# Chunk 3's diagonal sum taken one inner slice sooner, and its masks put ahead of two remainders, in a two-stage kernel (linear attention, then two mixtures of dense layers)

## The chip, the cores and the metric

One core of a Trainium2 chip runs the whole program. The engines named here are TensorE (PE, with its weight loads PEld), VectorE (DVE), ScalarE (ACT), GpSimd (POOL) and SyncE (SP, which here only issues DMAs). The metric is device time in microseconds (us) from the start to the end of one execution; lower is better.

## The reference, cut to what matters

The input is a linear attention with decay over B=2, H=8, S=768, D=48; its output x (1536 tokens by 384) goes through four experts of width 1024, each weighted by a normalised probability, and then through a dense layer of width 2048 with an ELU.

```python
# attention, per head, step t (d, e: 48 by 48 state)
cur   = (u * k[t])[:, None] * v[t][None, :]
y[t]  = r[t] @ (state + cur)
state = w[:, None] * state + k[t][:, None] * v[t][None, :]
# experts
p = probs / probs.sum(-1)
for e in range(4): out += p[:, e] * (relu(x @ w1[e]) @ w2[e])
# last layer
h = out @ w_in;  g = where(h > 0, h, exp(min(h, 0)) - 1);  return g @ w_out
```

## The kernel before

**Chunks of the attention.** The 768 steps of each of the two sequences are cut in 6 chunks of 128, so there are chunks 0 to 11. r and k of a chunk arrive transposed (tile `rkT`) and are scaled on VectorE by powers of w, two instructions for a chunk (`scale`, L231). TensorE then forms the products k·r of the whole chunk (`s2`, L297, 32 small matmuls) in two PSUM banks. What is above the diagonal is kept and put into a table `A` by two masked copies on VectorE (`s2p`, L304, "the masks" below). The diagonal of `A` is another quantity: u·k·r summed over a head. GpSimd multiplies (`s1u`, L248 and L250, tile `uk`), VectorE sums (L256, the "diagonal sum", tile `a0`), and the sums are spread over a diagonal table, one half of the heads by GpSimd (`s1g`, L260) and the other by ScalarE (`s1e`, four instructions, L266). `s1d` is L256 and L260 together. The masks therefore need three things: `s2` of the chunk, L260 and L266.

**Row of a chunk.** `s3(c)` puts together the output of chunk c: r times the carried state (L368), then, as `more` is set, `s2(c+1)`, then the chunk's own contribution to the state (`s3u`, L319, into a `ph` bank), then `A` times v (L380, 16 matmuls, which need the masks of chunk c). VectorE adds the state (`s3s`, L340), ScalarE copies the output to `yT` (L392), and `s3w` (L352, ScalarE) multiplies the new state by the decay of a chunk. After each odd chunk the pair goes out to HBM (`xd`, two DMAs, L397) and comes back in token layout (`xs`, L401), and `s4` splits it in a high and a low part `xh`, `xl` (L542, L543) for the experts. `s2(c+1)` uses the same two PSUM banks as `s2(c)`, so its first two matmuls wait for the two masked copies of chunk c.

**Experts.** Each float matrix product is made of three products of rounded high and low parts. `layers` runs over expert `u`, a block of tokens `t0`, and an inner slice `f` of 128 hidden units (8 slices). For u=0 the first two blocks have 256 tokens. In a slice, `st1` makes 9 matmuls into a `ph` bank (L742), `evac` lets ScalarE take relu (`hh`, L756) and VectorE the remainder (`hl`, L757), and `st2` of the slice two before makes 9 more (L782). At the end of a slice, `work(0.9)` splits one weight slice: ScalarE rounds it (`wh`, L588), VectorE forms the rest (`wl`, L589), and SP is told to load the raw slice that takes the freed buffer. There are three raw buffers and eight weight slices for u=0; two are split before `layers` begins, and one at the end of each inner slice from then on (#2 in slice 0, #3 in slice 1, and so on).

**What sets the order.** The program runs under a manual schedule: every engine takes its instructions in the order in which the code emits them, and so does SP with its DMAs. The attention is woven into the first three token blocks of u=0 by a table, `plan`, with keys (t0 // 256, f, early). An early entry (E) runs between `st1` and `evac`, a late one (L) between `evac` and `st2`:

```python
after = before(u, t0, f)
ph = self.st1(u, t0, n, f)
if after: after(True)                     # E
pend.append((..., *self.evac(u, n, ph)))
if after: after(False)                    # L
if first: self.st2(*first)
if not u or not BA <= f <= BB: self.work(0.9 if not u else 1.2)
```

In the kernel before, slice 1 (entry `y2`, late) holds row 2, the loads of chunk 5, all of chunk 3's diagonal (`diag(3)` is `s1d`, `s1e` and `s3w`), its keys and the scaling of chunk 4, and then split #3. Slice 2 holds, late, `s2(3)` and the masks of chunk 3. Slice 3 holds row 3 (`out(3)`, with `s2(4)` in it), slice 4 chunk 4's diagonal, masks and keys, slice 5 the scaling of chunk 5, slice 6 chunk 5's diagonal and row 4, slice 7 the scaling of chunk 6 and `s4(3)`, whose `xh` and `xl` the next block's first `st1` reads. `s1u(c+1)`, the product that chunk c+1's sum reads, is part of `keys(c)`.

Of the kernel before, what the change touches and what calls it, by code (L numbers as in the profile page):

```python
# [36 lines left out]
BA, BB = 1, 2  # L37
# [487 lines left out]
class Gen:  # L525
# [364 lines left out]
    def layers(self, tb0, before):  # L890


        pend = []
        for u in range(NU):

            m = 0 if u else 2 * tb0
            for t0, n in [(t, tb0) for t in range(0, m, tb0)] + [(t, TB) for t in range(m, N, TB)]:
                for f in range(NF):
                    after = before(u, t0, f)
                    ph = self.st1(u, t0, n, f)  # L900
                    if after:
                        after(True)
                    first = pend.pop(0) if len(pend) >= (2 if u < NE else 3) else None

                    if first and first[3] == NF - 1:
                        self.st2(*first)
                        first = None
                    pend.append((u, t0, n, f, *self.evac(u, n, ph)))
                    if after:
                        after(False)  # L910
                    if first:
                        self.st2(*first)
                    self.run_later()
                    if not u or not BA <= f <= BB:
                        self.work(0.9 if not u else 1.2)
                    if 0 < u < NE and t0 == 0 and f == 2:
                        self.load_pb(u)
        u, t0, n, f, hh, hl = pend[-1]
        for k, i in ((0, 0), (1, 0), (0, 1), (1, 1), (2, 0), (2, 1), (0, 2), (1, 2), (2, 2)):
            self.st2i(*pend[k], i)  # L920
            if k == 2:
                self.evac2i(u, t0, n, i)
# [13 lines left out]
    def fast(self):  # L936
        tc, nc = self.tc, self.nc
        with ExitStack() as ctx:
            self.setup(ctx)
            actx = ExitStack()  # L940
            at = Fast(self, actx)
# [4 lines left out]
            dp = self.probs_in()  # L946
# [76 lines left out]
            def scale(c):  # L1023
                at.s1h(c, 0)
                at.s1h(c, 1)

            def loads(c):
                load(c)
                if c < NCH:
                    at.load_rk(c)  # L1030

            def diag(c):
                at.s1d(c)
                at.s1e(c)
                at.s3w()

            def keys(c):
                at.s1k(c)
                if c + 1 < NCH:
                    at.s1u(c + 1)  # L1040
# [8 lines left out]
            def y2(c):  # L1049
                at.s3(2)  # L1050
                loads(5)
                self.probs_out(lambda: self.pop.tile([P, TB], F32, tag="po0", name="po0"))
                diag(3)
                keys(3)
                scale(4)

# [9 lines left out]
            def rest(c):  # L1066
# [4 lines left out]
            pb = lambda c: self.load_pb(0, *((0, TB), (TB, N))[c])  # L1071
            E, L = True, False
            plan = {
                (0, 0, L): [(lambda c: self.probs2(dp), 0), (k2, 2), (scale, 3)],
                (0, 1, L): [(y2, 2)], (0, 2, L): [(at.s2, 3), (at.s2p, 3)], (0, 3, L): [(out, 3)],
                (0, 4, L): [(diag, 4), (at.s2p, 4), (keys, 4)], (0, 5, E): [(scale, 5)], (0, 5, L): [(pb, 0)],
                (0, 6, E): [(diag, 5)], (0, 6, L): [(out, 4)],
                (0, 7, E): [(scale, 6)], (0, 7, L): [(at.s4, 3), (diag, 6)], (1, 0, L): [(out, 5)],
                (1, 1, E): [(scale, 7)], (1, 1, L): [(diag, 7)], (1, 2, L): [(out, 6)],
                (1, 3, E): [(scale, 8)], (1, 3, L): [(at.s4, 5), (diag, 8)], (1, 4, L): [(out, 7)],  # L1080
# [118 lines left out]
```

## Time and profile before

| | us |
|---|---|
| median of 3 runs | 657.28 (657.26 to 657.31) |
| the profiled execution, its own time | 655.06 |
| its span, first to last instruction | 653.2 |
| TensorE busy | 639.8 (98%) |
| VectorE, ScalarE, GpSimd busy | 327.9, 234.3, 197.6 |
| mean granted TensorE clock | 0.995 of full |

A timeline row gives the start and the duration of an instruction (or of several of one kind, with their count), its engine and line, what it writes and reads, and in brackets the idle time of its engine just before it with what ended that idle time. A window row gives the busy time of each engine in a stretch and the granted clock of TensorE (1.00 is 2.4 GHz, 0.50 is 1.2 GHz). Instructions of one engine overlap by some tens of ns, so that the next one starts a little before the last one's end. Matmul ends are modelled.

### The profile page before, as it was taken

How to read it: one execution, taken by the hardware profiler on the slowest of the kernel's cores; microseconds unless marked ns; L12 is line 12 of the kernel's file. 1: busy time of each engine (PE TensorE's matmuls, PEld its weight loads, DVE VectorE, ACT ScalarE, POOL GpSimd, SP SyncE). 2: the span in 40 equal slices, each digit the busy share in tenths (PEclk: the TensorE clock that was granted, in tenths of full speed). 3: DMA queues.
4: the chain of work that ended last, by engine and by line, in shares of the span. 5: the costliest groups of instructions: out<-in, count | busy, mean ns of one | idle time of the engine just before them, and what ended most of it. 6: DMA issues, size and time to landing. Idle time of an engine off the chain costs nothing.

```text
span 653.2 us, 9220 instructions
## 1 busy us (share of the span) xinstructions
PE 639.8 (98%) x3699; PEld 532.0 (81%) x3701; DVE 327.9 (50%) x452; ACT 234.3 (36%) x438; POOL 197.6 (30%) x169
## 2 busy tenths in 40 slices
PE   8789999999999999999999999999999999999997
PEld 6678988888888888888888888888888888888885
DVE  7856652355454555554545455566676753112122
ACT  7544443233211122211122112123546464544442
POOL 8734541000012130311130314142764434333331
PEclk9989999999999999999999999999999999999999
DMA  8973552433220224322207232208540342001011
GB/s 244 284 223 112 164 153 99 159 98 121 97 96 2 96 82 137 121 98 96 97 2 264 75 121 94 96 25 314 194 146 25 121 145 97 0 1 50 1 49 53
DMA packets 27736, 72.70 MB, mean 111 GB/s; under 512 B 3283, under 2 KB 8453, under 8 KB 27685
## 3 DMA queue, kind: packets, MB, share of 16 engines
q1 hardware_dynamic: 22784, 59.41, 28.3%
q10 hardware_dynamic: 4900, 12.61, 5.0%
q8 instruction: 31, 0.51, 0.3%
q14 instruction: 21, 0.16, 0.1%
HBM read 55.08 MB, written 16.93 MB: 110 GB/s over the span
## 4 chain that ended last, share of the span: by engine, by line
PE 93%; DMA 3%; DVE 1%; ACT 1%; issue 1%; SPq 0%; DVEq 0%; ACTq 0%
PE ph L742 44%; PE po L782 44%; DMA raw<-in_ws_dram 3%; PE pa L297 1%; PE po L927 1%; PE pa L380 1%; PE ph L319 1%; DVE rkT L231 1%; PE pa L368 1%; PE po L380 0%; SPq L551 0%; ACT A L266 0%; DVE A L304 0%; ACT wS L352 0%; ACT wh L588 0%
## 5 line engine op out<-in xcount | busy, mean ns | idle before, releaser
L742 PE MATMUL ph<-xh,wh 128*128 128x512 f32 (+1 forms) x456 | 171.5, 379 | 0.5 <-ACT xh L542 0.3
L742 PE MATMUL ph<-xh,wl 128*128 128x512 f32 (+1 forms) x456 | 170.9, 378 | 0.0
L782 PE MATMUL po<-hh,wh 128*128 128x512 f32 (+1 forms) x447 | 169.7, 380 | 0.0
L782 PE MATMUL po<-hh,wl 128*128 128x512 f32 (+1 forms) x447 | 168.8, 378 | 0.0
L782 PE MATMUL po<-hl,wh 128*128 128x512 f32 (+1 forms) x447 | 168.8, 378 | 0.0
L756 ACT ACTIVATE hh<-ph 128x512 fp32r<-128x512 f32 (+1 forms) x104 | 58.6, 563 | 255.0 <-PE ph L742 254.8
L757 DVE SCALAR_TENSOR_TENSOR hl<-ph,hh 128x512 fp32r<-128x512 f32 (+1 forms) x104 | 67.4, 648 | 161.5 <-ACT hh L756 161.5
L742 PE MATMUL ph<-xl,wh 128*128 128x512 f32 (+1 forms) x456 | 123.1, 378 | 0.0
L742 PEld LDWEIGHTS ph<-xh,wh 128*128 128x128 f32 x456 | 85.7, 188 | 17.1 <-ACT xh L542 1.0
L742 PEld LDWEIGHTS ph<-xh,wl 128*128 128x128 f32 x456 | 85.8, 188 | 15.8
L769 POOL TENSOR_TENSOR hl<-g,hh 128x512 fp32r<-128x512 f32 x48 | 63.0, 1314 | 117.7 <-ACT hh L768 109.5
L782 PEld LDWEIGHTS po<-hh,wh 128*128 128x128 f32 x447 | 84.0, 188 | 17.1 <-issue 1.5
L782 PEld LDWEIGHTS po<-hl,wh 128*128 128x128 f32 x447 | 84.0, 188 | 15.6
L782 PEld LDWEIGHTS po<-hh,wl 128*128 128x128 f32 x447 | 84.0, 188 | 15.6
L742 PEld LDWEIGHTS ph<-xl,wh 128*128 128x128 f32 x456 | 83.4, 188 | 16.2 <-DVE xl L543 0.2
L652 POOL TENSOR_TENSOR nl<-a,wide 128x768 fp32r<-128x768 f32 x16 | 29.8, 1864 | 188.0 <-DVE a L651 147.2
L766 DVE SCALAR_TENSOR_TENSOR g<-m,ph 128x512 f32<-128x512 f32 x48 | 32.9, 686 | 104.5 <-ACT m L764 99.1
L804 POOL TENSOR_TENSOR acc<-acc,t 128x512 f32<-128x512 f32 x27 | 34.2, 1297 | 72.9 <-DVE t L803 72.9
L768 ACT CAST hh<-g 128x512 fp32r<-128x512 f32 x48 | 29.9, 622 | 43.0 <-DVE g L766 43.0
L763 ACT ACTIVATE m<-ph 128x512 f32<-128x512 f32 x48 | 28.7, 598 | 43.4 <-PE ph L742 36.7
L589 DVE TENSOR_TENSOR wl<-raw,wh 128x768 fp32r<-128x768 f32 x32 | 31.0, 981 | 9.1 <-ACT wh L588 8.6
L764 ACT ACTIVATE m<-m 128x512 f32<-128x512 f32 x48 | 30.3, 632 | 1.5
(134 smaller groups left out, 496.0 us busy)
## 6 DMA issues: line engine op xcount, KB each, us to landing
raw<-in_ws_dram SPq DMA_DIRECT2D x32, 384.0 KB, 4.1
wide<-in_ws_dram SPq DMA_DIRECT2D x16, 768.0 KB, 5.1
w<-nh ACTq DMA_DIRECT2D x16, 384.0 KB, 2.4
w<-nl ACTq DMA_DIRECT2D x16, 384.0 KB, 5.6
wh<-w SPq DMA_DIRECT2D x16, 384.0 KB, 6.2
wl<-w SPq DMA_DIRECT2D x16, 384.0 KB, 6.8
rk<-in_rkv_dram SPq DMA_DIRECT2D x12, 384.0 KB, 5.5
rkT<-in_rkT_dram SPq DMA_DIRECT2D x10, 448.0 KB, 5.4
```

The source lines that it names most:

```text
L589: self.weng.tensor_tensor(out=lo, in0=t, in1=hi.bitcast(F32), op=ALU.subtract)
L652: nc.gpsimd.tensor_tensor(out=lo, in0=af, in1=cf, op=ALU.add)
L742: nc.tensor.matmul(ph[:, 0:n], a[:, kk, c0:c0 + P], b[:, kk], start=q == 0, stop=q == 3 * KD - 1)
L756: nc.scalar.activation(hh[:, 0:n], ph[:, 0:n], AF.Relu)
L757: nc.vector.scalar_tensor_tensor(out=hl[:, 0:n], in0=ph[:, 0:n], scalar=0.0, in1=hh[:, 0:n].bitcast(F32), op0=ALU.max, op1=ALU.subtract)
L763: nc.scalar.activation(m, ph, AF.Relu, scale=-1.0)
L764: nc.scalar.activation(m, m, AF.Exp, scale=-1.0)
L766: nc.vector.scalar_tensor_tensor(out=gg, in0=m, scalar=-1.0, in1=ph, op0=ALU.add, op1=ALU.max)
L768: nc.scalar.copy(hh, gg)
L769: nc.gpsimd.tensor_tensor(out=hl, in0=gg, in1=hh.bitcast(F32), op=ALU.subtract)
L782: nc.tensor.matmul(po, a[:, ff, i * P:(i + 1) * P], b[:, 0:n], start=f == 0 and q == 0 and not i * n % TB, stop=f == NF - 1 and q == 2 and ...
L804: nc.gpsimd.tensor_tensor(out=a, in0=a, in1=t[:, 0:n], op=ALU.add)
```

## The change

Nothing is computed differently; the order of emission changes in the first token block.

- Slice 0, late: `s1d(3)` (sum of chunk 3's diagonal, and GpSimd's half of the table) is added behind the scaling of chunk 3. In slice 1 only `s1e(3)` and `s3w` are left of `diag(3)`.
- Slice 1: no split at its end. Every later split is one slice later: #3 at the end of slice 2, #4 of slice 3, up to #7 of slice 6.
- Slice 2: `s2(3)` and chunk 3's masks are early, so the masks stand ahead of the slice's relu remainder and of the rest of split #3.
- Slice 3: `diag(4)` follows row 3 directly, before `st2` and the split.
- Slice 4: chunk 4's masks and keys are early; the scaling of chunk 5 comes late in this slice and no longer early in the next one.
- Slice 5, late: `diag(5)`, which was early in slice 6.

```diff
-                    if not u or not BA <= f <= BB:
+                    if (t0 or f != 1) if not u else not BA <= f <= BB:
                         self.work(0.9 if not u else 1.2)
...
                 self.probs_out(lambda: self.pop.tile([P, TB], F32, tag="po0", name="po0"))
-                diag(3)
+                at.s1e(3)
+                at.s3w()
                 keys(3)
                 scale(4)
...
-                (0, 0, L): [(lambda c: self.probs2(dp), 0), (k2, 2), (scale, 3)],
-                (0, 1, L): [(y2, 2)], (0, 2, L): [(at.s2, 3), (at.s2p, 3)], (0, 3, L): [(out, 3)],
-                (0, 4, L): [(diag, 4), (at.s2p, 4), (keys, 4)], (0, 5, E): [(scale, 5)], (0, 5, L): [(pb, 0)],
-                (0, 6, E): [(diag, 5)], (0, 6, L): [(out, 4)],
+                (0, 0, L): [(lambda c: self.probs2(dp), 0), (k2, 2), (scale, 3), (at.s1d, 3)],
+                (0, 1, L): [(y2, 2)], (0, 2, E): [(at.s2, 3), (at.s2p, 3)], (0, 3, L): [(out, 3), (diag, 4)],
+                (0, 4, E): [(at.s2p, 4), (keys, 4)], (0, 4, L): [(scale, 5)], (0, 5, L): [(diag, 5), (pb, 0)],
+                (0, 6, L): [(out, 4)],
```

## Rows read from the trace of the kernel before

**Rows 1.** The page: busy time of the engines, share of the span, instructions.

```profile
PE 639.8 (98%) x3699; PEld 532.0 (81%) x3701; DVE 327.9 (50%) x452; ACT 234.3 (36%) x438; POOL 197.6 (30%) x169
```

**Rows 2.** Windows: stretch, length, busy PE PEld DVE ACT POOL, PEclk, DMA, GB/s.

```profile
27.99:31.49 3.50, 0.01 (x3) 0.01 (x1) 2.73 (x4) 2.02 (x5) 3.25 (x3) 1.00 0.91 247
31.49:36.18 4.69, 4.51 (x65) 3.76 (x65) 2.07 (x4) 0.37 (x1) 0.00 (x0) 0.64 0.81 268
...
46.01:50.08 4.07, 4.07 (x64) 3.55 (x65) 2.46 (x6) 1.81 (x6) 2.24 (x3) 0.58 0.73 224
...
60.00:120.00 60.00, 59.85 (x669) 51.98 (x668) 28.07 (x50) 23.02 (x65) 21.04 (x19) 1.00 0.47 141
```

**Rows 3.** Timeline of TensorE, first token block.

```profile
20.65 0.67 PE L319 MATMUL po<-v,kp 128*64 128x48 f32 x16
...
22.50 0.29 PE L714 MATMUL po<-ident,pn 128*48 128x128 f32 x1
...
23.96 1.10 PE L297 MATMUL pa<-rkT 48*64 48x128 f32 x32
...
31.49 0.43 PE L297 MATMUL pa<-rkT 48*64 48x128 f32 x2 [3.49 <-DVE A L304]
...
36.18 0.39 PE L782 MATMUL po<-hh,wh 128*128 128x256 f32 x1
...
38.43 0.28 PE L782 MATMUL po<-hh,wh 128*128 128x256 f32 x1
...
46.01 1.98 PE L297 MATMUL pa<-rkT 48*64 48x128 f32 x32 [2.51 <-DVE rkT L231]
...
50.08 0.39 PE L782 MATMUL po<-hh,wh 128*128 128x256 f32 x1
...
54.75 0.62 PE L742 MATMUL ph<-xl,wh 128*128 128x256 f32 x3
```

**Rows 4.** Timeline of VectorE, same stretch.

```profile
22.37 1.50 DVE L231 TENSOR_TENSOR rkT<-rkT,Kd 112x512 f32<-112x512 f32 x1
...
25.25 0.54 DVE L256 TENSOR_REDUCE a<-uk 128x8 f32<-128x384 f32 x1
...
28.76 1.70 DVE L589 TENSOR_TENSOR wl<-raw,wh 128x768 fp32r<-128x768 f32 x1 [0.92 <-ACT wh L588]
30.39 0.41 DVE L757 SCALAR_TENSOR_TENSOR hl<-ph,hh 128x256 fp32r<-128x256 f32 x1
30.72 1.31 DVE L304 COPY_PREDICATED A<-mask,pa 128x512 f32<-128x512 uint8 x2
31.94 0.93 DVE L589 TENSOR_TENSOR wl<-raw,wh 128x768 fp32r<-128x768 f32 x1
```

**Rows 5.** Timeline of ScalarE, same stretch.

```profile
25.82 1.28 ACT L266 ACTIVATE A<-ident,a 128x128 f32<-128x128 f32 x4 [2.65 <-DVE a L256]
27.01 1.00 ACT L352 ACTIVATE wS<-S,T 112x48 f32<-112x48 f32 x4
27.91 0.82 ACT L588 CAST wh<-raw 128x768 fp32r<-128x768 f32 x1
...
36.33 0.37 ACT L392 COPY yT<-po 112x256 f32<-112x256 f32 x1 [0.18 <-PE po L380]
```

**Rows 6.** Timeline of GpSimd, same stretch.

```profile
21.75 1.56 POOL L250 TENSOR_TENSOR uk<-uk,rk 128x384 f32<-128x384 f32 x1
```

**Rows 7.** Timeline of SP's DMA issues.

```profile
36.73 0.83 SPq L397 DMA_DIRECT2D xd<-yT  x2
41.62 0.39 SPq L401 DMA_DIRECT2D xs<-xd  x1
```

**Rows 8.** DMA issues of the span: KB each, median us to landing.

```profile
raw<-in_ws_dram SPq DMA_DIRECT2D x32, 384.0 KB, 4.1
...
pb<-pd SPq DMA_DIRECT2D x1, 512.0 KB, 8.9
```

**Rows 9.** Waits of SP, 0 to 110 us: total, times, longest.

```profile
SPq L551 <- PE po L368: 11.0, 2, 10.0
```

## The prediction

> **What bounds the kernel now.** I read the page first: TensorE is busy 639.8 us of a span of 653.2 (98%) while VectorE, ScalarE and GpSimd are at 50%, 36% and 30% [rows 1]. So at most some 13 us are to be had, and the windows say where. From 60 us on TensorE is full (59.85 of 60.00) at a granted clock of 1.00 [rows 2]; what is lost lies before that, in the first token block, the block that the diff rearranges. The TensorE timeline shows two standstills there: 3.49 us until 31.49, released by VectorE's masks, and 2.51 us until 46.01, released by VectorE's scaling [rows 3]. Each is followed by a stretch at a lowered clock: 0.64 on average from 31.49 to 36.18, 0.58 from 46.01 to 50.08 [rows 2], a mix of the levels 1.2 and 2.4 GHz. The third view is the timelines of the other engines: which instruction stood in front of the masks. Since everything behind 60 us is full, I carry a time won at the end of block one to the end of the kernel one to one.
>
> What a lowered clock costs: products of a chunk (32 matmuls) take 1.10 us [rows 3], of which 1.04 up to the next start; state share plus A times v take 22.50 - 20.65 = 1.85 [rows 3]. That is 2.9 us, against 4.69 and 4.07 in the two stretches [rows 2]. The first holds a second short wait of about 0.5 (two matmuls, then the second masked copy), so the clock cost about 1.2 in each, 2.4 together.
>
> **The change part by part.** No instruction, DMA or split is added or removed; the sum is one of queues. I give new times in the frame of the profiled execution.
>
> *Chunk 3's masks.* Before, VectorE finished the scaling of chunk 4 at 28.76 - 0.92 = 27.84, waited 0.92 for ScalarE's rounding, and then did the rest of split #3 (1.63 up to the next start) and a relu remainder (0.33) before the masks at 30.72 [rows 4]. In the new order these three stand behind the masks. The diagonal sum (0.54, some 0.46 of it up to the next start) only moves from behind to ahead of rest #2, remainder and state, so the scaling of chunk 4 starts at the same time; it ends some 0.1 later, because GpSimd's table is now beside its first half. Masks: 27.95, that is 2.8 earlier. What else do they need? The sum follows the scaling of chunk 3, which ends at 22.37 + 1.50 = 23.87, and its product was ready at 21.75 + 1.56 = 23.31 [rows 4, 6]; so the sum is there at 24.35, ScalarE's half of the table (1.28, [rows 5]) at 25.7, GpSimd's at about 26.1, the products at 23.96 + 1.10 = 25.06 [rows 3]. All are done 1.8 us before the masks: VectorE's queue is the last wait. Rest #2 comes half a microsecond later, about 25.2, when TensorE wants it at 25.3: nothing.
>
> *Row 3.* Its products start after the first masked copy, 27.95 + 0.7 = 28.7, go on after the second, 29.3, and end at 30.4; then 1.85: row 3 ends at 32.2, against 36.18 [rows 3]. 2.8 of these 4.0 us are the masks, 1.2 the clock, which I take not to fall: TensorE now stands 0.7 and 0.5 us, far from the 3.49 and 2.51 that preceded the two falls. If it falls all the same, 1.2 is lost again.
>
> *What is late next: split #4.* It is one slice later, and on ScalarE it now stands behind row 3's copies and chunk 4's table and decay. The second copy of row 3 started at 36.33 [rows 5], now at 32.3; then 0.3 (copy), 1.2 (table), 0.9 (decay), 0.8 (rounding), all up to the next start: 35.5. The rest takes 0.93 alone [rows 4], but stands next to GpSimd's product for chunk 5 (35.0 to 36.0 by the same count: table, keys, two products of 1.0 each from 32.0 on). Beside such a product the row of 22.37 took 1.50 where its twin takes 0.67, and the product 1.56 [rows 4, 6]; so 0 to 0.8 extra, and I take 0.4: rest #4 is there at 36.8. TensorE reaches this `st2` at 34.4 (32.2, then eighteen matmuls at 0.12, from the steps of 36.18 to 38.43) and can make two matmuls of the nine without the rest. It goes on as if the group had begun at 36.6; before, it began at 38.43 [rows 3]. Of the 4.0 us, 2.2 are given back here.
>
> *Up to row 4.* From 38.43 to 46.01 TensorE worked 7.58 - 2.51 = 5.07 us [rows 3]. VectorE meanwhile: masks 4 (1.3), remainder 0.3, scaling of chunk 5 (1.3), rest #5 (0.9) from 36.8 to 40.5, and TensorE wants rest #5 at 40.0: 0.5 of waiting. Row 4's products start at 36.6 + 5.07 + 0.5 = 42.2, and nothing holds them: scaling 5 is done at 39.6, masks 4 at 38.1. So the standstill of 2.51 and its clock (1.2) go. They end with A times v 2.9 later, at 45.1, against 50.08 [rows 3]: 5.0 ahead.
>
> *End of the block.* The low part of the next block's x is VectorE's last in a row: after rest #5, remainder (0.3) and sum of chunk 5 (0.5) to 41.3; ScalarE's table (1.2) and rounding #6 (0.8) to 43.3; rest #6 with a wait of 0.9 behind GpSimd's product for chunk 6, to 45.2; remainder 0.3, state 0.3, masks 1.3, rest #7 0.9, scaling 1.3, remainder 0.3, low part 0.96: 50.3. TensorE would be there at 50.1 - 0.7 = 49.4, since its way from 50.08 to 54.75 was 4.67 with 0.3 of waits [rows 3]. So the three matmuls of 54.75 start at 50.3: 4.4 us earlier. From there both orders are the same.
>
> *SP's queue.* Raw #6 is issued behind rest #3, 30.7 (it was 30.5). Raw #7 falls behind the loads of chunk 6, `xd` and `xs`; `xs` waits for `xd` to land, 41.62 - 36.73 = 4.9 from first issue [rows 7], so raw #7 goes out at about 38 and lands at 42 by the median 4.1, at 46.9 by the longest row, 8.9 [rows 8]. ScalarE wants it at 45.5, with 1.5 us of slack up to VectorE's use. I take nothing. Chunk 5's product (GpSimd, from 34.0) finds its data shortly before; late by 0.5, it costs 0.5.
>
> **The sum.** The profiled execution: 655.06 - 4.4 = 650.7. The median of the runs shown is 2.2 above that execution, and the rows don't say where; I take the same 4.4 off: 652.9. Differences under 0.2% (1.3 us) can't be told from none.
>
> **The rivals.**
> *The clock falls all the same (15%).* TensorE stands 1.1 and 1.1 us between 34.4 and 36.9, with two matmuls between. The rows hold no such pair: against a fall speaks the half of work left, for it that 2.51 us sufficed at 43.50. One fall costs 1.2, two 2.4: 654.1 to 655.3.
>
> *GpSimd loses the race (10%).* GpSimd has the table of chunk 5 and a first product (1.0 each) from 41.3 on, so its second product asks at 43.3, as rest #6 does; which goes first is a toss-up within the precision of this count. If VectorE's does, the low part comes 0.9 earlier and TensorE no longer waits for it: 652.0. The Trainium skill (SBUF — State Buffer, "Who interferes with whom") says that a VectorE operation with two SBUF inputs and a GpSimd one that reads SBUF exclude each other for a whole instruction, and that issue order decides who is blocked; by it, too, this race would end at 652.0 or at the forecast and nowhere between. The trace agrees that one waits for the other (1.50 instead of 0.67 beside 1.56).
>
> *The masks come no earlier (10%).* If something that the timelines don't show releases the masks (a table half, the second bank), they stay at 30.72: 2.8 goes and one clock fall of 1.2 stays, 4.0 of the 4.4. Time 656.9, no change that can be told. For it: VectorE worked nearly without a pause before them. Against: the 1.8 us of margin above.
>
> *Slower: raw #7 holds ScalarE (6%).* Its rounding stands ahead of slice 7's relu and of `xh` on ScalarE, and with these the next block. Each us that it lands after 46.9 is one us of the kernel; it is slower than before from a landing after 51.3. SP's queue has been held for 10.0 us by one of its own waits [rows 9]; held as long here, raw #7 lands at 42.7 + 10 = 52.7 and costs 5.8: 658.7. For it: `xd` and `xs` stand in front of it in the same queue. Against: 4.8 us of room before any loss at the median landing.
>
> **How the numbers follow.** Forecast 59%, clock 15%, race 10%, masks no earlier 10%, raw #7 6%. Faster by over 0.2%: 59 + 15 + 10 = 84%; within 10%; slower 6%. The forecast's own range is 651.8 to 654.0 (rest #4 with 0 to 0.8 of waiting, a product late by 0.5). The whole range goes from 651.0 (race won, and the median's 2.2 partly of the same standstills) to 655.8 (two falls and half a microsecond); the last two rivals lie outside.
>
> **What would show it.** Masks of chunk 3 at 28 with VectorE idle under 0.2 before them; products of chunk 4 at about 28.7, clock 1.00 behind them; a new wait of about 2 us at the `st2` of slice 4 released by a rest (L589); no wait at the products of chunk 5; a wait under 1 us at the `xl` matmuls, which start near 50.3. It is wrong if TensorE's first long wait is still for L304 after 31, if the clock is under 1.00 between 32 and 50, or if SP or ScalarE waits on a raw slice near 46.

## The result, and the profile after

The changed kernel takes 649.96 us (median of 4, 649.39 to 651.72) against 657.29 (4 runs): ratio 0.9891, 95% interval 0.9871 to 0.9911, so 5.8 to 8.5 us less. In a second set of runs it was 651.06 against 656.52, ratio 0.9914 (0.9900 to 0.9927), 4.8 to 6.6 less. Forecast: 652.9, range 651.0 to 655.8. The direction and the mechanism were right; the size was too small, and the first result lies 1.0 below the range. The profiled execution took 650.08 us with a granted clock of 1.0.

TensorE's timeline of the changed kernel, first token block (start, duration, what, idle before), answers to [rows 3]:

```profile
24.53 1.10 PE L297 MATMUL pa<-rkT 48*64 48x128 f32 x32
...
29.33 0.43 PE L297 MATMUL pa<-rkT 48*64 48x128 f32 x2 [0.64 <-DVE A L304]
29.94 1.10 PE L297 MATMUL pa<-rkT 48*64 48x128 f32 x30 [0.18 <-DVE A L304]
30.96 0.61 PE L319 MATMUL ph<-v,kp 128*64 128x48 f32 x15
...
32.43 0.39 PE L782 MATMUL po<-hh,wh 128*128 128x256 f32 x1
...
35.81 0.39 PE L782 MATMUL po<-hh,wh 128*128 128x256 f32 x1 [0.96 <-ACT wh L588]
...
37.15 0.39 PE L782 MATMUL po<-hh,wl 128*128 128x256 f32 x1 [0.84 <-DVE wl L589]
...
42.43 1.04 PE L297 MATMUL pa<-rkT 48*64 48x128 f32 x32
...
44.87 0.39 PE L782 MATMUL po<-hh,wh 128*128 128x256 f32 x1
...
49.74 0.62 PE L742 MATMUL ph<-xl,wh 128*128 128x256 f32 x3 [0.22 <-DVE xl L543]
```

The 3.49 us in front of chunk 4's products are 0.64, the 2.51 in front of chunk 5's are gone, and the new wait for split #4 stands at the `st2` of slice 4 (0.96 for its rounding, 0.84 for its rest). The windows, answering to [rows 2], show a full clock in both rows (chunk 3's and chunk 4's), and the same 59.85 of 60 us further on:

```profile
28.69:29.33 0.64, 0.00 (x0) 0.00 (x1) 0.64 (x2) 0.04 (x1) 0.64 (x1) 1.00 0.83 259
29.33:32.43 3.10, 2.92 (x64) 2.33 (x64) 3.10 (x6) 0.31 (x1) 1.16 (x2) 1.00 1.00 255
42.43:44.87 2.44, 2.44 (x72) 2.08 (x64) 1.26 (x3) 1.69 (x5) 2.36 (x3) 1.00 0.94 327
60.00:120.00 60.00, 59.85 (x607) 51.63 (x607) 26.26 (x45) 22.38 (x61) 18.68 (x17) 1.00 0.48 149
```

VectorE of the changed kernel, answering to [rows 4]: the masks follow the scaling of chunk 4 without a gap, rests #3, #4 and #6 (L589) come behind, and the low part of x (L543) ends at 49.68.

```profile
27.13 1.50 DVE L231 TENSOR_TENSOR rkT<-rkT,Kd 112x512 f32<-112x512 f32 x1
28.56 1.32 DVE L304 COPY_PREDICATED A<-mask,pa 128x512 f32<-128x512 uint8 x2
...
30.11 1.28 DVE L589 TENSOR_TENSOR wl<-raw,wh 128x768 fp32r<-128x768 f32 x1
...
35.79 1.31 DVE L589 TENSOR_TENSOR wl<-raw,wh 128x768 fp32r<-128x768 f32 x1 [3.29 <-ACT wh L588]
...
43.61 0.96 DVE L589 TENSOR_TENSOR wl<-raw,wh 128x768 fp32r<-128x768 f32 x1 [2.07 <-ACT wh L588]
...
48.74 0.94 DVE L543 TENSOR_TENSOR xl<-xs,xh 128x768 fp32r<-128x768 f32 x1
```

**Where the time comes from.** Cut each profiled execution at two points: the start of chunk 3's products (24.53 above) and that of the three `xl` matmuls (49.74). What lies behind the second is 600.2 to 600.8 us in every kernel of this study, so start and stage explain the differences to within 0.6 us.

| kernel | start | stage | profiled time | clock |
|---|---|---|---|---|
| before, the profile shown | 23.96 | 30.79 | 655.06 | 0.995 |
| before, second profile | 24.73 | 31.38 | 656.50 | 0.992 |
| before with fillers (below) | 25.25 | 28.07 | 653.54 | 1.0 |
| changed | 24.53 | 25.21 | 650.08 | 1.0 |
| changed, second profile | 25.33 | 25.60 | 651.11 | 0.999 |
| first half of the change | 24.29 | 26.22 | 650.93 | 0.998 |
| second half of the change | 24.52 | 28.80 | 653.84 | 0.994 |
| changed, sum back in slice 1 | 24.23 | 25.07 | 649.53 | 1.0 |
| changed, split of slice 1 kept | 24.21 | 26.99 | 651.47 | 0.993 |
| changed, one more copy | 25.08 | 25.88 | 651.40 | 1.0 |
| changed, two splits in slice 2 | 24.25 | 24.52 | 648.95 | 1.0 |
| changed, the whole better order | 24.37 | 22.97 | 648.17 | 1.0 |

The stage lost 5.58 us (forecast 4.45, from 54.75 - 23.96 to 50.3 - 23.96). Between the two profiles of the second set of runs it lost 31.38 - 25.60 = 5.78. The start, which no instruction of the change touches, differs by up to 1.4 us between executions, and the profile of before that I worked from is the earliest of all; why the starts differ was not tried.

### The profile page after: what moved, and what is told of

Read it like the earlier page. It is cut to its first block, busy times and chain, and to the rows that moved or that the text cites. A ratio compares the mean times of both kernels' runs of the same rounds, so it can differ in the third digit from the quotient of the medians.

```text
span 648.3 us, 9224 instructions
## 1 busy us (share of the span) xinstructions
PE 638.2 (98%) x3701; PEld 529.8 (82%) x3701; DVE 326.2 (50%) x452; ACT 234.4 (36%) x438; POOL 198.4 (31%) x169
## 4 chain that ended last, share of the span: by engine, by line
PE 92%; DVE 2%; DMA 2%; issue 1%; POOL 1%; ACT 1%; SPq 0%; DVEq 0%
PE ph L742 44%; PE po L782 44%; DMA rk<-in_rkv_dram 2%; PE pa L297 1%; PE po L927 1%; DVE rkT L231 1%; PE pa L380 1%; DVE A L304 1%; PE pa L368 1%; PE ph L319 0%; DVE wl L589 0%; PE po L380 0%; SPq L551 0%; POOL uk L250 0%; ACT wh L588 0%
## 5 line engine op out<-in xcount | busy, mean ns | idle before, releaser
L763 ACT ACTIVATE m<-ph 128x512 f32<-128x512 f32 x48 | 28.7, 598 | 43.4 <-PE ph L742 36.6
L589 DVE TENSOR_TENSOR wl<-raw,wh 128x768 fp32r<-128x768 f32 x32 | 31.1, 984 | 11.4 <-ACT wh L588 10.9
```

The lines of the kernel that those rows point to most:

```text
L589: self.weng.tensor_tensor(out=lo, in0=t, in1=hi.bitcast(F32), op=ALU.subtract)
L763: nc.scalar.activation(m, ph, AF.Relu, scale=-1.0)
```

## The experiments

Ratios are against runs of the kernel before in the same set of runs, each set on a chip of its own: medians 656.46 (the filled kernel, the two halves, two splits), 656.52 (the second set above: the two repetitions, the race, the better order) and 656.63 (the sum's place, the split kept). What was expected in us was reckoned from the 657.3 of the first set, some 0.8 higher; so where it is close, drops are compared and not times.

**The clock: the kernel before, its standstills filled.** In `s3`, ahead of row 3 and row 4, into the row's own bank:

```diff
...
+        for _ in range({3: 14, 4: 10}.get(ci, 0)):
+            nc.tensor.matmul(py[0], self.zero[:, 0:P], self.zero, start=True, stop=True)
...
```

> The kernel before with its order untouched, and with 14 and 10 matmuls of zeros by zeros (128x512, bf16) ahead of rows 3 and 4, into a bank that the row then overwrites: TensorE works through its two standstills and waits for nothing later than before. Theory clock: the queues alone are worth 1.9 to 2.8 us of the change, the rest of the 7.3 is TensorE's clock, which falls behind the two standstills for longer in the timed executions than in the profiled one; so this kernel comes to 652.5 to 653.5 with a granted clock of 1.0, and the runs of the kernel before show about 0.99. Theory standstill: the clock is the 2.4 us read off the profile and no more, and what is left is waiting; then it comes to 654.9. Theory neither (the filler is in the way): 657 or more.

653.40 (653.06 to 653.54), ratio 0.9953 (0.9939 to 0.9967), clock 0.999 to 1.0, while the 12 runs of the kernel before beside it showed 0.990 to 0.995 at 655.23 to 657.66. TensorE's timeline of this kernel (lines from 358 on are moved by three; the filler is L361): the rows still start when VectorE lets them, and waits of 0.48 and 0.34 are left, but they run at full clock.

```profile
25.25 1.10 PE L297 MATMUL pa<-rkT 48*64 48x128 f32 x32
...
28.54 3.19 PE L361 MATMUL pa<-zero 128*128 128x512 bf16 x14
...
32.79 0.43 PE L297 MATMUL pa<-rkT 48*64 48x128 f32 x2 [0.48 <-DVE A L304]
...
53.32 0.62 PE L745 MATMUL ph<-xl,wh 128*128 128x256 f32 x3 [0.34 <-DVE xl L546]
```

Its windows of row 3 and row 4; compare 31.49:36.18 and 46.01:50.08 of [rows 2], 4.69 and 4.07:

```profile
32.79:35.89 3.10, 2.92 (x64) 2.33 (x64) 2.08 (x4) 0.31 (x1) 0.00 (x0) 1.00 0.67 205
45.72:48.22 2.50, 2.50 (x64) 2.14 (x65) 1.60 (x3) 0.86 (x3) 0.75 (x1) 1.00 0.78 225
```

So the clock alone is 2.72 us of the stage (30.79 to 28.07) against the first profile and 3.31 against the second; by the ratio it is 2.2 to 4.0. The queues are the other 2.86 (28.07 to 25.21). That the clock costs this much without any change of order is shown; which of the two theories had its size is not. Reckoned from 657.3, theory clock is a drop of 3.8 to 4.8 and theory standstill one of 2.4; the measured drop is 3.1, and its interval reaches both.

**The kernel before, a second profile.**

> The kernel before once more, for a second profile of it. Theory clock: the executions of this kernel differ by how long the clock stays at 1.2 GHz behind the two standstills; a profile with a granted clock of 0.990 to 0.992 shows one or both of the stretches of 31 to 36 and 46 to 50 us twice as long at 0.5 as the profile shown, and rows that take up to 1 us longer in them, with everything from 60 us on the same. Rival: the clock is the same and something else (the start, a DMA, the end) is longer.

The two points of the table in it, and windows; compare the second window with 31.49:36.18 of [rows 2]:

```profile
24.73 1.10 PE L297 MATMUL pa<-rkT 48*64 48x128 f32 x32
...
56.11 0.62 PE L742 MATMUL ph<-xl,wh 128*128 128x256 f32 x3
```

```profile
28.76:32.26 3.50, 0.00 (x0) 0.00 (x1) 2.73 (x4) 2.01 (x5) 3.25 (x3) 0.78 1.04 258
32.26:37.50 5.24, 5.24 (x65) 4.23 (x65) 2.08 (x4) 0.37 (x1) 0.00 (x0) 0.50 0.83 269
44.83:47.34 2.51, 0.00 (x2) 0.00 (x0) 2.51 (x4) 0.44 (x1) 1.31 (x1) 1.00 0.97 197
47.34:51.45 4.11, 4.11 (x65) 3.58 (x65) 2.49 (x6) 1.92 (x6) 2.27 (x3) 0.58 0.59 194
```

The waits are the same, 3.50 and 2.51. But here the clock fell already within the first standstill (0.78 over it), and all of row 3 ran at 0.50: 5.24 us where the first profile has 4.69 from the end of its standstill. Of the 1.44 us by which this execution is slower, 0.59 is in the stage and 0.77 in the start. So theory clock holds for row 3 alone (row 4 took 4.11, as good as the 4.07 before), and the rival, a longer start, is the larger part.

**The changed kernel again.**

> The changed kernel once more, on the chip on which the next two run: 649.4 to 650.5 with a granted clock of 0.997 to 1.0.

651.06 (650.54 to 651.32), all five above what I expected; ratio 0.9914. The start is 0.8 later than in its first profile, and rest #4 lost to GpSimd's product this time: 1.25 instead of 0.84 at the `st2` of slice 4.

```profile
25.33 1.10 PE L297 MATMUL pa<-rkT 48*64 48x128 f32 x32
...
38.37 0.39 PE L782 MATMUL po<-hh,wl 128*128 128x256 f32 x1 [1.25 <-DVE wl L589]
```

```profile
36.59 1.72 DVE L589 TENSOR_TENSOR wl<-raw,wh 128x768 fp32r<-128x768 f32 x1 [3.29 <-ACT wh L588]
```

In the first profile GpSimd's first product for chunk 5 had waited 0.63 for its data, so that rest #4 met only the end of it and took 1.31; here the data was in time, and rest #4 had to let the second product pass:

```profile
35.28 1.00 POOL L248 TENSOR_TENSOR uk<-rk,ub 128x384 f32<-128x384 f32 x1 [0.63 <-DMA rk<-in_rkv_dram]
```

**One half each.** First half: slices 0 to 2 of the change with `plan` of before from slice 3 on. Second half: `plan` of the change from slice 3 on, all else as before.

```diff
# first half, against the changed kernel
+                (0, 3, L): [(out, 3)], (0, 4, L): [(diag, 4), (at.s2p, 4), (keys, 4)],
+                (0, 5, E): [(scale, 5)], (0, 5, L): [(pb, 0)], (0, 6, E): [(diag, 5)], (0, 6, L): [(out, 4)],
# second half, against the kernel before
+                (0, 3, L): [(out, 3), (diag, 4)], (0, 4, E): [(at.s2p, 4), (keys, 4)],
+                (0, 4, L): [(scale, 5)], (0, 5, L): [(diag, 5), (pb, 0)], (0, 6, L): [(out, 4)],
```

> Only the first half of the change: chunk 3's sum in slice 0, no split in slice 1, masks early in slice 2; slices 3 to 6 as in the kernel before. Theory masks: with the masks early everything behind them moves up, the second standstill goes too since the scaling of chunk 5 is done by then, and the time is that of the changed kernel, 650 within 0.7. Rival, chunk 4's order: the second standstill and its clock stay without the second half, 653 to 654.

> Only the second half: chunk 4's diagonal behind row 3, its masks and keys early in slice 4, scaling and sum of chunk 5 sooner; slices 0 to 2 as before. The first standstill of 3.5 us and the clock behind it stay, the second standstill shrinks to under 0.5. Theory clock: about half of the clock's loss goes and none of the queues' (rest #4 is no later, but the row comes at 31.5 as before): 654.5 to 655.5. Theory standstill: 2.5 us of waiting and 1.2 of clock go, 653.5.

First half: 651.32, ratio 0.9925 (0.9909 to 0.9940), clock 0.996 to 0.998; it holds most of the gain, and both standstills are gone; what it has instead is 1.77 us at the `st1` of slice 6, behind chunk 4's table on ScalarE, and 1.20 for the low part of x:

```profile
39.01 0.38 PE L742 MATMUL ph<-xh,wh 128*128 128x256 f32 x1 [1.15 <-ACT wh L588]
40.01 0.38 PE L742 MATMUL ph<-xh,wl 128*128 128x256 f32 x1 [0.62 <-DVE wl L589]
...
50.51 0.62 PE L742 MATMUL ph<-xl,wh 128*128 128x256 f32 x3 [1.20 <-DVE xl L543]
```

It is beyond the 0.7 that I gave theory masks around 650. The time alone doesn't exclude the rival (a drop of 3.9 to 6.0, where the rival's is 3.3 to 4.3); the trace does, since chunk 5's products wait 0.22 there, not 2.51. Second half: 653.84, ratio 0.9960 (0.9945 to 0.9975), clock 0.992 to 0.997. Its drop of 2.6 (1.6 to 3.6) is that of theory clock (1.8 to 2.8) and less than the 3.8 of theory standstill: chunk 5's products no longer wait, but new waits of 0.31, 0.71 and 0.33 for VectorE take part of it back. The first standstill stays and its row goes at half clock:

```profile
32.04 2.58 PE L297 MATMUL pa<-rkT 48*64 48x128 f32 x32 [3.49 <-DVE A L304]
```

**The sum's place, and the split of slice 1.**

```diff
# sum: s1d(3) back in slice 1
-                (0, 0, L): [..., (scale, 3), (at.s1d, 3)],
+                (0, 0, L): [..., (scale, 3)],
-                at.s1e(3); at.s3w()
+                diag(3)
# split: one at the end of slice 1 again
-                    if (t0 or f != 1) if not u else not BA <= f <= BB:
+                    if not u or not BA <= f <= BB:
```

> The changed kernel with the whole of chunk 3's diagonal left in slice 1. Theory: VectorE has the same instructions ahead of the masks in both orders and both halves of the table are done by 27.5, before the masks at 28: the sum's place is worth nothing, ratio 0.989 to 0.992 as the changed kernel. Rival: the table is then the last thing that the masks wait for, they come 0.5 to 1 us later and the ratio is 0.993 or more.

> The changed kernel with the split of slice 1 left in (one split a slice from slice 0 on, as before). Theory: what counts is that rest #3 no longer stands in VectorE's queue ahead of chunk 3's masks; with it there the masks come at 30.5, the first standstill is 3 us again with the clock at 1.2 GHz behind it, and only the second half's gain is left: 653.0 to 654.5, a ratio of 0.994 to 0.997, granted clock under 0.998. Rival: the early place in slice 2 (ahead of the remainder) is what counts, and the time is that of the changed kernel within 0.7.

The sum's place is worth nothing that can be told: 649.87, ratio 0.9903 (0.9888 to 0.9918). The split's was a miss of mine: 650.72, ratio 0.9916 (0.9902 to 0.9930), not to be told from the change. VectorE's timeline of that kernel says why:

```profile
28.23 0.95 DVE L589 TENSOR_TENSOR wl<-raw,wh 128x768 fp32r<-128x768 f32 x1
29.10 1.33 DVE L304 COPY_PREDICATED A<-mask,pa 128x512 f32<-128x512 uint8 x2
```

With the sum a slice sooner ScalarE's rounding is ready in time, so VectorE no longer waits 0.92 for it, and rest #3 went ahead of GpSimd (0.95, not 1.70 as in [rows 4]). The masks come only 0.87 later. So the time fits the rival, but for another reason than the remainder's 0.33. With either edit alone VectorE no longer waits for rounding #3 ahead of the masks; the early masks with neither edit were not run. The standstill is 1.53 here, and that is enough for the clock in some executions; with the split moved and the sum back it is 0.55. One row of each kernel:

```profile
29.89 2.58 PE L297 MATMUL pa<-rkT 48*64 48x128 f32 x32 [1.53 <-DVE A L304]
```

```profile
28.81 0.43 PE L297 MATMUL pa<-rkT 48*64 48x128 f32 x2 [0.55 <-DVE A L304]
```

Five runs of the kernel with the split kept: 650.23 and 650.40 at a clock of 0.999 to 1.0, 650.72 at 0.996, 651.47 and 651.93 at 0.993. So leaving out the split buys no queue time that can be told, but a standstill short enough for the clock.

**GpSimd's race.** One more copy of 128x384 on ScalarE ahead of split #6:

```diff
+            def hold(c):
+                t = at.c.tile([P, DM], F32, name="hold")
+                nc.scalar.copy(t, at.ub)
...
-                (0, 5, L): [(diag, 5), (pb, 0)],
+                (0, 5, L): [(diag, 5), (hold, 0), (pb, 0)],
```

> The changed kernel with one more ScalarE copy (128x384) ahead of split #6's rounding, so that rest #6 asks 0.4 us later, behind GpSimd's second product for chunk 6. Theory: rest #6 waits for the whole of that product, VectorE's chain to the low part of x ends 0.9 to 1.3 us later, and TensorE waits for it there: 650.6 to 651.4. Rival, VectorE has room at that place and the race is worth nothing: 649.7 to 650.3.

651.68, ratio 0.9929 (0.9915 to 0.9942); beside the changed kernel of the same set 0.6 more, with intervals that overlap, so the time alone decides nothing. The trace shows that the theory's wait is there, and about half its price: rest #6 now waits and takes 1.57 instead of 0.96, and the `xl` matmuls wait 0.69 instead of 0.21 or 0.22. Rest #4 won its race in this execution (0.49 of waiting instead of 0.84), which hid part of the price.

```profile
44.23 1.57 DVE L589 TENSOR_TENSOR wl<-raw,wh 128x768 fp32r<-128x768 f32 x1 [2.48 <-ACT wh L588]
```

```profile
50.96 0.62 PE L742 MATMUL ph<-xl,wh 128*128 128x256 f32 x3 [0.69 <-DVE xl L543]
```

**Split #4 sooner, and a better order.** First only `self.work(1.8)` (two splits) at the end of slice 2; then also chunk 4's masks late, chunk 5's sum behind slice 6's remainder, and the scaling of chunk 6 behind the low part of x:

```diff
+                        self.work((0.9 if t0 or f != 2 else 1.8) if not u else 1.2)
# the second kernel also
+                (0, 4, L): [(at.s2p, 4), (keys, 4), (scale, 5)], (0, 5, L): [(pb, 0)],
+                (0, 6, L): [(diag, 5), (out, 4)],
+                (0, 7, L): [(at.s4, 3), (scale, 6), (diag, 6)],
```

> The changed kernel with two splits at the end of slice 2, so that split #4 is made while ScalarE waits for row 3, and each later split in its old slice. Theory: the two waits of 0.96 and 0.84 us at the st2 of slice 4 go, and the one for rest #5 in slice 6; VectorE then ends the low part of x 1.1 us earlier than in my count of the changed kernel, but only 0.2 to 0.5 earlier than its trace has it: 649.3 to 649.8. Rival, VectorE's queue is not the bound there and TensorE's 2 us are won whole: 648.0.

> The changed kernel with two splits at the end of slice 2 (so split #4 fills ScalarE's wait for row 3), chunk 4's masks behind slice 4's remainder, chunk 5's sum behind slice 6's relu and remainder, and the scaling of chunk 6 behind the low part of x. By the count of queues TensorE's waits at the st2 of slice 4, at the st1 of slices 6 and 7 and at the low part go, 2.5 us against the changed kernel's trace, of which the wait for xh on ScalarE stays: 647.5 to 648.2. Rival, the waits move to the next instruction in VectorE's queue, as in the run with two splits: 649.2 or more.

Two splits: 649.54, ratio 0.9898 (0.9879 to 0.9917), 0.4 below the first result of the changed kernel, though in another set of runs, and its stage is 0.7 shorter (24.52): VectorE's queue takes most of the 1.80 back, the waits return at the `st1` of slices 6 and 7 (0.85 and 0.70).

```profile
38.65 0.39 PE L742 MATMUL ph<-xh,wh 128*128 128x256 f32 x1 [0.85 <-DVE hl L757]
...
44.88 0.39 PE L742 MATMUL ph<-xh,wh 128*128 128x256 f32 x1 [0.70 <-DVE hl L757]
```

The whole order: 648.53, ratio 0.9878 (0.9863 to 0.9894), against 0.9914 for the changed kernel of the same set: 2.5 us less, the best of this study, though 0.3 over what I expected. Its stage is 22.97; of the waits there are left 0.65, 0.18, 0.18 and one of 0.40 for the scaling of chunk 5:

```profile
39.99 1.10 PE L297 MATMUL pa<-rkT 48*64 48x128 f32 x32 [0.40 <-DVE rkT L231]
```

## Why the prediction was right and where it was wrong

**Right: the masks and what follows.** The start of the changed profile is 0.57 later than that of before; taking this off, the masks came at 27.99 (forecast 27.95), the products at 28.76 and 29.37 (28.7, 29.3), rest #4 at 36.5 (36.8), chunk 5's products at 41.9 without a wait (42.2). The new wait at the `st2` of slice 4 was 1.80 (about 2). "VectorE's queue is the last wait" holds: moving the sum back changed nothing.

**Mis-sized: row 3 and the clock.** The step took 1.85 for the state's share and A times v; at full clock they took 32.43 - 30.96 = 1.47 here. With 0.38 too much in the undisturbed price, the clock's loss came out too small, 1.2 a standstill. The windows of the filled kernel give 4.69 - 3.10 = 1.59 for row 3 and 4.07 - 2.50 = 1.57 for row 4; of these 3.2 its stage keeps 2.72, against the 2.4 of the forecast, mostly since TensorE then waits for the low part of x (0.34). In the changed kernel the shorter row brought rest #4 0.3 sooner than forecast.

**Wrong way round: the race.** In the step "End of the block" rest #6 was to wait 0.9 behind GpSimd's product, with 10% for the other outcome, though I called the race a toss-up. The other outcome came: rest #6 went first, 0.96 in the row above, and GpSimd's product took the wait. GpSimd's timeline of the changed kernel:

```profile
43.77 1.67 POOL L250 TENSOR_TENSOR uk<-uk,rk 128x384 f32<-128x384 f32 x1
```

The low part of x ended at 49.1 by the same count instead of 50.3. The race is the larger part of the 1.1 us by which the stage beat the forecast. The Trainium skill (SBUF — State Buffer, "Who interferes with whom") has it that issue order decides who is blocked; the rows agree, 0.96 in the order that won and 1.57 in the run that was held back. The last section has a row that does not: there GpSimd had begun first and was passed.

**Wrong: the base.** "The median of the runs shown is 2.2 above that execution, and the rows don't say where; I take the same 4.4 off." This is the step that failed. It added 2.2 us to the forecast, and those are most of the 2.9 by which the forecast lies above the result; the 1.1 of the stage adds to it, the start of the changed profile, 0.57 later, takes off, and the rest is under 0.2. Only the lower end of the range had taken some of the 2.2 off.

What the runs showed in its place: the execution from which all terms were read was the milder of the two that were profiled, with the earlier start and the shorter fall of the clock, and nearly the fastest of its kernel. Of the 30 timed runs of before in the three later sets one (654.94) lies below its 655.06; the 22 with a clock of 0.988 to 0.992 took 656.7 in the mean, the 8 with 0.993 to 0.995 took 655.7. The changed kernel's profiled execution (650.08) was no such case beside its median of 649.96. The change removes the fall in whatever length it comes, so by this reading, which no trace of the first set can test, a typical execution had more to give than the 4.4 that this one showed. The second profile shows 0.59 us of this in the stage; for the three runs of the first median no trace is left, so how their 2.2 us divide between start and clock stays open (of the 7.3 us won there the stage of the two profiles accounts for 5.6). In the second set the gain is 656.52 - 651.06 = 5.46, about what the stage lost there; the changed kernel lies inside the range there by 0.06, from a base that is 0.8 lower, so that is no confirmation of the 4.4.

**The rivals.** The clock did not fall in the changed kernel's profile (its runs have 0.997 to 1.0). But the argument against a fall, that the gaps were far from 2.51, was weaker than I put it: 1.53 sufficed in the run with the split kept. The pair of gaps that I feared was there (0.96 and 0.84, in the second profile 0.96 and 1.25, two matmuls between), and in both profiles the clock was 1.00 over it and behind it. The masks came early, so that rival is out; "GpSimd loses the race" is what happened. Raw #7 held nobody, by a hair. The changed kernel's SP issues:

```profile
33.64 0.87 SPq L397 DMA_DIRECT2D xd<-yT  x2
40.92 0.39 SPq L401 DMA_DIRECT2D xs<-xd  x1
41.40 0.44 SPq L551 DMA_DIRECT2D raw<-in_ws_dram  x1
```

`xs` waited 7.3 us behind `xd` instead of the 4.9 of [rows 7], so raw #7 left at 41.4 and not 38; landing took 3.9, and ScalarE read it at 45.35. Two of the prediction's sums have no row behind them: raw #7 lands at 42 in the step and at 42.7 in the rival (from 42 the rival is 658.0, not 658.7), and the 50.1 in "50.1 - 0.7" is not derived (45.1 + 4.67 - 0.3 gives 49.5, near its 49.4). Neither changes the forecast.

## What to carry to other kernels

A standstill of TensorE that is followed by a low granted clock costs its own length and, here, 1.6 to 2.1 us more in the row behind it (4.69 and 5.24 against 3.10, 4.07 against 2.50); filling it with matmuls of zeros separates the two prices without touching the order. Before a forecast is set against a median, look whether the profiled execution is a typical one: where its time is below that of the timed runs, what it shows as lost may be less than they lose. And when an instruction is taken out of the way of one wait, follow its queue to the next buffer that it holds: an earlier split and three reorderings further down were worth another 2.5 us.

## What the runs showed of the hardware that was not expected

- The same standstill has different prices: behind 3.49 to 3.50 us of idle TensorE, row 3 took 4.69 us in one execution and 5.24 in another, since the clock fell after the work had resumed in the one and before it in the other. Behind 1.53 us the clock fell in the profiled execution, and the five runs of that kernel show 0.993 twice, 0.996, 0.999 and 1.0. Not all of a lower mean is such a fall: in three profiles the clock is 0.94 to 0.96 over the last 19 to 20 us of the kernel (first half, split kept, second profile of the changed kernel), and what lies behind the second point of the table is no longer there (600.2 to 600.4).
- An operation of GpSimd can lose to VectorE twice in a row: the first product for chunk 4 (L248), 1.0 us alone, took 2.33 in the run with the split kept, while the end of chunk 4's scaling and then rest #3 went ahead of it, although rest #3 began only at 28.23:

```profile
27.72 2.33 POOL L248 TENSOR_TENSOR uk<-rk,ub 128x384 f32<-128x384 f32 x1
```

- The time from the program's start to chunk 3's products varies from 23.96 to 25.33 us over the profiled executions, although the order up to there is nearly the same in all.
